# The last keys of two head groups as one pass of 64x32 tiles in an attention and feed-forward kernel

## The chip, the cores and the metric

The kernel runs on one core of a Trainium2 chip. The metric is the device time of one execution in microseconds, the median of several runs. The core has five engines that run their own queues in order and meet at semaphores: TensorE (PE) multiplies, VectorE (DVE) and ScalarE (ACT) work on tiles, GpSimd (POOL) issues most loads, SyncE (SP) issues most stores. TensorE writes its results to PSUM, which has eight banks here; the program calls them `banks`.

## The reference

```python
batch, n_heads, seq, head_dim = (8, 12, 448, 64)
scores = scale * np.matmul(q, k.transpose(0, 1, 3, 2))
scores = scores - np.max(scores, axis=-1, keepdims=True)
attn = np.exp(scores)
attn = attn / (np.sum(attn, axis=-1, keepdims=True) + 1e-09)
x = np.matmul(attn, v)          # then heads side by side: 3584 x 768
h = x @ w_in                    # 768 x 2048
g = h * (1.0 / (1.0 + np.exp(-h)))
return g @ w_out                # 2048 x 768
```

The sizes that matter below are the 448 keys of a head, which are three and a half chunks of 128, and the 448 queries, which are the columns that every attention matmul streams.

## The kernel before

**Units and pairs.** Four heads of one batch make a head group, `HG = 4`; each batch has three, so there are 24 units, numbered n. Units are taken in pairs (n, n+1), n even. For one unit the keys lie in chunks c = 0 to 3; the last chunk holds only 64 keys. The two units of a pair share it: unit n has its 64 keys on rows 0 to 63, unit n+1 on rows 64 to 127, and one exponentiated tile E holds both (`lead[n+1] = n` leads the second unit to the first one's tile).

**The attention work on TensorE.** A score pass (`scores`, recorded at L583) uses tiles of 32 rows and 128 columns of the array, one for each head, so four matmuls run side by side. The shared last chunk's scores (`scores_rest`) use 32x64 tiles, eight side by side. Sums and values (`attend`, L674 for the sums of a pair, L658 for values) use 128x32 tiles: four heads side by side, each on 32 columns of the array. I call a pass what runs side by side: four matmuls of 128x32 or 32x128, eight of 32x64, one of 128x128. A unit's value work is in two parts, one for the even and one for the odd elements of the head dimension; a part has four passes, one for each chunk, that add up in one bank. In the last of them the unit reads all 128 rows of the shared tile, and its V buffer holds zeros on the 64 rows that belong to the other unit. Those rows are cleared once per buffer by DVE (`clear_rows`, L468).

**The rest of TensorE's work.** The feed-forward products (`wide`, L573) use the full array, 128x128, or, while attention is still going on and the planner's clock is past `STRIPS`, four 128x32 strips for each product, so that they have the same tile size as the value passes. `FFN1_AT` is how many of the six passes of one first-layer product are put down at once before the planner looks for other work. From the middle of batch 4 on the first layer of two batches is done by a scheme with fewer products (L909); some weight combinations for it are made on DVE in good time (`TWB`, `SXB` are their priorities).

**Order.** The order of each engine's instructions is written out ahead of time by a planner, a small simulation (`Order`, and the loop at the end of `without_maximum`) with costs for each operation: a pass of n columns is n/2400 us plus 2.6 ns, a change of the array's tile size is `SWITCH = 0.104`. On TensorE it prefers a score pass if one is due and its spacing (`PACES`, one value for each unit) has elapsed; then any sum or value work that is ready; then feed-forward work. Right behind a score pass it puts all sum and value work that is ready:

```python
while n0 >= NG and (a := av_at()) is not None and a <= od.now:
    run_av()
```

Four of the eight banks are a ring `m_ring` that values, sums and feed-forward products share (the two scores in flight hold the other four). A value part takes one bank and gives it back when DVE has scaled it into xT (`norm`, L756). The E tiles are a ring of nine; a unit's are given back with its second value part. V buffers are a ring of four, given back at the same place, and POOL's next V load waits for that. The `B_...` values are priorities on ACT and DVE.

The sequence of sum and value operations of a pair is: the sums of both, then for unit n parts 1 and 2, then for unit n+1 parts 1 and 2:

```python
av_seq.append((ns, 0))
av_seq += [([n], part) for n in ns for part in (1, 2)]
```

Of the kernel before, what the change touches and what calls it, by code (L numbers as in the profile page):

```python
# [22 lines left out]
DMA_TAIL = 2.2  # L23
OPEN = 8
TS = (1, 3)
STRIPS = 50
W_LATE = 1.0
LAND = {1: -1.0, 2: -0.9, 3: -0.2, 4: 0.45, 5: 1.2, 6: 1.2, 7: 1.2, 8: 1.2, 9: 1.0, 10: 0.9, 11: 0.8, 12: 0.8}

# [1 line left out]
def mm(n):  # L31
    return n / 2400.0 + 0.0026
# [331 lines left out]
def without_maximum(  # L364
# [16 lines left out]
    HG = 4  # L381
# [11 lines left out]
    NT = 2 * S // 128  # L393
    OH = DM // 2
    NRK, NRQ, NKT, NV, NTH = 3, 4, 3, 4, 2
    PACES = (0.0, 0.0, 0.0, 1.6, 1.2, 2.0, 1.2, 1.2, 1.2, 1.2, 0.8, 1.8, 1.2, 1.2, 1.2, 1.2, 1.8, 1.8, 0, 0, 0.8, 0.8, 0.8, 2.5)
    B_TURN, B_ADD, B_GATE, B_TANH, B_WSUM, B_GSUM, B_FOURTH = 5, 5.5, -9, 11.2, 10, 2.5, 0
    B_NORM, B_INV, B_TAKE, B_READ = -10, -10, 1, -3.5
    LONES = ()
    NPL = 4  # L400
    HALVES = 4
# [2 lines left out]
    MORE0 = 4  # L404
    COLD, FIRST = 8.5, 39
    SHY = 0.3
    TWB, SXB, FAR = 12, 4, 20
    NE, NX3, NT_ = 9, 8, 2
    NXT = 3 * NX3
    NSG, NTMP, NOST = 3, 3, 4  # L410
# [18 lines left out]
    def bank_m(*key):  # L429
        return bank_of(4 + spot[key])  # L430
# [28 lines left out]
    VS = [const.tile([128, HG, NCH, D], FP16, name=f"V{i}") for i in range(NV)]  # L459

    def clear_v(i):
        f = form(i // NG, i % NG)
        before = form((i - NV) // NG, (i - NV) % NG) if i >= NV + NG else None
        return f != "lone" and f != before and i < B * NG
# [35 lines left out]
    def form(b, hg):  # L500
        n = NG * b + hg
        if n in LONES:
            return "lone"
        return ("low", "high")[(n - sum(x < n for x in LONES)) % 2]
# [87 lines left out]
    def per_burst(n):  # L592
        return 1
# [19 lines left out]
    def rows_of(n, c):  # L613
        return KROWS[c] if form(*units[n][:2]) == "lone" else 128
# [35 lines left out]
    def attend_mm(a, n, part, c, h, k0, k1, e, start, stop):  # L650
        b, hg, g0, g1 = units[n]
        nq = 32 * (g1 - g0)
        at = nq * (c % per_burst(n))
        if part == 0:
            w = side[:, n % 2] if n < 4 and c == NCH - 1 else ones[k0:k1, :]
        else:
            w = v_of(b, hg)[k0:k1, h + HG * hg * (b == 0), c, part - 1 :: 2]
        nc.tensor.matmul(  # L658
            out=a[32 * h : 32 * (h + 1), 0:nq],
            lhsT=w,  # L660
            rhs=e[k0:k1, h, at : at + nq],
            start=start,
            stop=stop,
        )
# [17 lines left out]
    def attend(ns, part):  # L682
        if part == 0 and len(ns) == 2:
            attend_sums(ns)
            return
        for n in ns:
            a = bank_m("a", n, part)
            acc[(n, part)] = a
            if part == 0 and n in TS:
                for i, (w, e) in enumerate(  # L690
                    ((ones, T[n]), (side[:, n % 2], E[(lead.get(n, n), NCH - 1)]))
                ):
                    for h in range(HG):
                        nc.tensor.matmul(  # L694
                            out=a[32 * h : 32 * (h + 1), 0:S],
                            lhsT=w,
                            rhs=e[:, h, 0:S],
                            start=(i == 0),
                            stop=(i == 1),
                        )  # L700
                continue
            if part == 0 and n < FOLD:
                nq = 32 * (units[n][3] - units[n][2])
                for w in range(2):
                    kr = rows_of(n, 2 * w)
                    for h in range(HG):
                        nc.tensor.matmul(
                            out=a[32 * h : 32 * (h + 1), 0:nq],
                            lhsT=ones[0:kr, :],
                            rhs=T[n][0:kr, h, nq * w : nq * (w + 1)],  # L710
                            start=(w == 0),
                            stop=(w == 1),
                        )
                continue
            for c in range(NCH):
                e = E[(lead.get(n, n) if c == NCH - 1 else n, c // per_burst(n))]
                for h in range(HG):
                    attend_mm(a, n, part, c, h, 0, rows_of(n, c), e, c == 0, c == NCH - 1)

    def inverse(ns, step, i=0):  # L720
        g0, g1 = units[ns[0]][2:]
# [476 lines left out]
    inv_op, norm_op = [], []  # L1198
    quads, fourth, begun = [], [], []

    PROD_AT, FFN1_AT = 1, 2

    def in_parts(n, size, columns, emit, done, at=0):
        to = min(at + size, n)
# [411 lines left out]
    for ns in jobs:  # L1616
        if len(ns) == 1:
            split = ((0,), (1,)) if ns[0] < HALVES else ((0, 1),)
            qk_seq += [(ns, c, ys) for c in range(NCH // per_burst(ns[0])) for ys in split]
        else:  # L1620
            split = ((0,), (1,)) if ns[0] < HALVES else ((0, 1),)
            each = [[([n], c, ys) for c in range(NCH - 1) for ys in split] for n in ns]
            if ns[0] == 0 and len(split) == 2:
                each[0].sort(key=lambda x: x[2])
            if ns[0] < 4:
                qk_seq += each[0] + [(ns, 3, (0, 1))] + each[1]
                av_seq += [([n], part) for n in ns for part in range(3)]
                lead[ns[-1]] = ns[0]
                continue
            qk_seq += each[0] + each[1] + [(ns, 3, (0, 1))]  # L1630
        av_seq.append((ns, 0))
        av_seq += [([n], part) for n in ns for part in (1, 2)]
        lead[ns[-1]] = ns[0]
    pace = {"next": 0.0}
    av_data = {"at": None}
# [97 lines left out]
    def av_at():  # L1733
        if not av_seq:
            return None
        ns, part = av_seq[0]
        if len(ns) == 2 and part == 0:
            if any(len(t_op.get(n, ())) < 2 or len(exp_op[n]) < 8 for n in ns):
                return None
            deps = [t_op[ns[0]][1], (t_op[ns[1]][1], mm(S))]  # L1740
            deps += [(x, 2 * mm(S)) for x in exp_op[ns[0]][6:8]]
            at, m = when(deps), m_ring.when(1)
            av_data["at"] = at
            return None if at is None or m is None else max(at, m)
        deps, b = [], units[ns[0]][0]
        for n in ns:
            if len(exp_op.get(n, ())) < 2 * NCH // per_burst(n):
                return None
            nq = 32 * (units[n][3] - units[n][2])
            if part == 0 and n in TS:  # L1750
                if len(t_op.get(n, ())) < 2:
                    return None
                deps += t_op[n] + [(x, mm(nq)) for x in exp_op[n] if x not in own_exp(n)]
                continue
            if part == 0 and n < FOLD:
                if len(t_op.get(n, ())) < 2:
                    return None
                deps += [t_op[n][0], (t_op[n][1], mm(nq))]
                continue
            made = exp_op[n][2:] + exp_op[n][:2] if n in (1, 3) else exp_op[n]  # L1760
            for i, x in enumerate(made):
                c = i // 2 * per_burst(n)
                deps.append((x, c * mm(nq)))
            if part:
                deps += [(x, LATE * (b == 0)) for x in ld_v[units[n][:2]]]
                if b > 0:
                    deps += [(x, 1.2) for x in rdn_op.get(n, [None])]
        at = when(deps)
        av_data["at"] = at
        m = m_ring.when(len(ns))  # L1770
        if at is None or m is None:
            return None
        return max(at, m)

    def run_av():
        ns, part = av_seq.pop(0)
        b, hg, g0, g1 = units[ns[-1]]
        nq = 32 * (g1 - g0)
        two = len(ns) == 2
        spot[("a", ns[0], part)] = m_ring.take()[0]  # L1780
        if part == 0:
            mms = 3 if two else 2 if ns[0] < FOLD or ns[0] in TS else 4
        else:
            mms = 4
        op = Op(
            "PE",
            mms * mm(nq) + 0.013,
            lambda: attend(ns, part),
            tail=PE_OUT,
        )  # L1790
        if part == 2:

            def then(at):
                n = ns[0]
                for _ in range(NCH // per_burst(n) - (lead.get(n + 1) == n)):
                    e_ring.give(at)
                b, hg = units[n][:2]
                if b:
                    v_ring.give(at)
                i = NG * b + hg + NV  # L1800
                if b and i < B * NG and clear_v(i):
                    od.add(Op("DVE", 0.2, lambda: clear_rows(i), [op], 5))

            op.then = then
        elif part == 0 and (two or ns[0] < FOLD or ns[0] in TS):
            op.then = lambda at: [t_ring.give(at) for _ in ns]
        od.on_pe(op, "cols")
        if part == 0:
            after_sums(ns, op, nq)
        else:  # L1810
            for n in ns:
                after_av(n, part, op, nq)
# [161 lines left out]
```

## Time and profile before

| | before |
|---|---|
| median of 3 runs | 383.17 us (383.01 to 383.21) |
| the profiled execution | 382.61 us |
| its span | 381.1 us |
| PE busy | 374.5 us, 98% |
| DVE busy | 280.7 us, 74% |
| ACT busy | 257.6 us, 68% |
| granted TensorE clock | 0.997 |
| score passes L583 | 768 matmuls |
| value matmuls L658 over E and V | 672 |

In the lists of the profile a row is one stretch of instructions of the same line and operands: when it starts, how long it lasts, engine, line, operation, what it writes and reads, the tile of the array (rows x columns, as in 128*32), the operand, and how many there are. The ends of matmuls are modelled, so durations overlap the next row; what a stretch costs is read from start to start.

### The profile page before, as it was taken

What the parts mean: (1) busy time and instruction counts of PE and PEld (TensorE: products, weight loads), DVE (VectorE), ACT (ScalarE), POOL (GpSimd) and SP (SyncE); (2) the same over time, 40 slices, a digit from 0 to 9 for tenths busy, and PEclk for the clock granted to TensorE, in tenths of its full rate; (3) what the DMA queues carried; (4) which work ended last, traced back from release to release, by engine and by line L of the source; (5) the groups of instructions that cost most, each with busy time, mean ns of one, the idle gap of its engine ahead of it and who ended that gap; (6) DMA issues with size and microseconds to landing.
All of it is one profiled execution on the core that took longest, in us unless ns stands there. A gap on an engine that the chain in (4) does not pass through costs nothing.

```text
span 381.1 us, 12970 instructions
## 1 busy us (share of the span) xinstructions
PE 374.5 (98%) x5516; PEld 192.7 (51%) x5516; DVE 280.7 (74%) x562; ACT 257.6 (68%) x425; POOL 91.0 (24%) x160
## 2 busy tenths in 40 slices
PE   8999999999999999999999999999999999999994
PEld 6433455444555444445544454555555555556553
DVE  5679799999996868996879978889876334656441
ACT  4998854787867797967788786738762259882221
POOL 7527515406042603324240500030001000000000
PEclk9999999999999999999999999999999999999998
DMA  7999999936558743739491702120002330001433
GB/s 109 202 206 196 185 210 183 154 74 94 74 98 134 137 71 46 103 76 170 81 143 26 98 23 67 34 54 0 1 7 70 83 93 2 0 1 45 107 80 109
DMA packets 35999, 34.73 MB, mean 91 GB/s; under 512 B 12000, under 2 KB 35168, under 8 KB 35936
## 3 DMA queue, kind: packets, MB, share of 16 engines
q0 software_dynamic: 25232, 22.82, 40.4%
q1 hardware_dynamic: 10176, 10.53, 10.4%
q8 instruction: 45, 0.74, 0.8%
q10 hardware_dynamic: 528, 0.49, 0.5%
q14 instruction: 18, 0.15, 0.1%
HBM read 45.61 MB, written 11.01 MB: 149 GB/s over the span
## 4 chain that ended last, share of the span: by engine, by line
PE 95%; ACT 3%; DVE 1%; DMA 1%; issue 0%
PE banks L573 54%; PE banks L909 15%; PE banks L583 11%; PE banks L658 10%; ACT E L621 2%; PE banks L1853 2%; PE banks L979 2%; PE banks L674 2%; DMA out_dram<-ost 1%; DVE T L632 0%; PE banks L694 0%; DVE ost L1061 0%; DVE ost L1052 0%; ACT ost L1050 0%; DVE zeros L436 0%
## 5 line engine op out<-in xcount | busy, mean ns | idle before, releaser
L621 ACT ACTIVATE E<-banks 128x896 f16<-128x896 f32 x168 | 144.0, 919 | 41.1 <-PE banks L583 40.8
L573 PE MATMUL banks<-xT,w_in_t 128*32 128x448 f16 (+1 forms) x1446 | 90.5, 353 | 0.0
L573 PE MATMUL banks<-w_out_t,G 128*32 128x384 f16 (+1 forms) x968 | 67.4, 327 | 0.0
L573 PEld LDWEIGHTS <-G 128*32 128x32 f16 (+1 forms) x1240 | 47.0, 97 | 34.0 <-issue 6.5
L573 PEld LDWEIGHTS <-w_in_t 128*32 128x32 f16 (+1 forms) x1446 | 42.2, 97 | 43.2 <-issue 12.7
L519 POOL DMA_DIRECT2D V<-in_v_dram x84 | 46.0, 559 | 56.6 <-PE banks L658 42.9
L583 PE MATMUL banks<-rq,KT 32*128 32x448 f16 (+1 forms) x768 | 52.4, 363 | 0.3 <-ACT E L621 0.2
L782 ACT ACTIVATE th<-banks 128x448 f16<-128x448 f32 x72 | 37.1, 552 | 15.1 <-PE banks L573 13.2
L820 DVE SCALAR_TENSOR_TENSOR G<-th,banks 128x448 f16<-128x448 f16 (+1 forms) x72 | 39.8, 572 | 4.8 <-ACT th L782 4.5
L1043 ACT COPY ost<-banks 128x384 f32<-128x384 f32 x41 | 19.8, 485 | 33.1 <-PE banks L573 17.9
L573 PE MATMUL banks<-D,S 128*32 128x384 f16 (+1 forms) x544 | 38.1, 327 | 0.0
L942 ACT ACTIVATE G<-banks 128x448 f16<-128x448 f32 (+3 forms) x72 | 33.8, 553 | 5.3 <-DVE banks L925 3.5
L658 PE MATMUL banks<-E,V 128*32 128x448 f16 x672 | 35.7, 353 | 0.0
L756 DVE SCALAR_TENSOR_TENSOR xT<-banks,rdn 128x448 f16<-128x448 f32 x48 | 29.2, 618 | 5.6 <-PE banks L658 3.0
L925 DVE TENSOR_TENSOR banks<-banks,q 128x448 f32<-128x448 f32 x28 | 17.6, 633 | 15.7 <-PE banks L909 14.5
L573 PEld LDWEIGHTS <-S 128*32 128x32 f16 (+1 forms) x544 | 20.6, 97 | 14.7 <-issue 3.1
L496 POOL DMA_DIRECT2D rq<-in_q_dram x25 | 13.9, 557 | 58.9 <-PE banks L583 46.9
L632 DVE TENSOR_TENSOR T<-E,E 128x1792 f16<-128x1792 f16 x22 | 23.8, 1080 | 5.6 <-ACT E L621 5.5
L632 DVE TENSOR_TENSOR T<-T,E 128x1792 f16<-128x1792 f16 x22 | 23.9, 1085 | 5.2 <-ACT E L621 5.1
L583 PEld LDWEIGHTS <-KT 32*128 32x128 f16 (+1 forms) x768 | 12.4, 96 | 29.9 <-issue 27.2
L658 PEld LDWEIGHTS <-V 128*32 128x32 f16 x672 | 17.0, 97 | 16.0 <-issue 3.9
L909 PEld LDWEIGHTS <-w_in_t 128*128 128x128 f16 x168 | 16.4, 98 | 15.2
(163 smaller groups left out, 409.3 us busy)
## 6 DMA issues: line engine op xcount, KB each, us to landing
out_dram<-ost SPq DMA_DIRECT2D x200, 48.0 KB, 1.6
rk<-in_k_dram POOLq DMA_DIRECT2D x23, 224.0 KB, 5.8
rq<-in_q_dram POOLq DMA_DIRECT2D x23, 224.0 KB, 5.2
w_out_t<-in_moe_w_out_dram POOLq DMA_DIRECT2D x4, 768.0 KB, 13.1
V<-in_v_dram POOLq DMA_DIRECT2D x42, 64.0 KB, 4.4
V<-in_v_dram POOLq DMA_DIRECT2D x42, 48.0 KB, 4.6
w_in_t<-in_moe_w_in_dram POOLq DMA_DIRECT2D x3, 512.0 KB, 10.8
w_in_t<-in_moe_w_in_dram POOLq DMA_DIRECT2D x6, 256.0 KB, 6.3
```

The source lines that it names most:

```text
L519: nc.gpsimd.dma_start(out=v_of(b, hg0)[32 * x : 32 * (x + 1), at, 0:count, :], in_=v[b, hs].rearrange("h (i g) d -> i h g d", g=TPP)[:, :, ...
L573: nc.tensor.matmul(out=out[at], lhsT=lhsT[:, at], rhs=rhs, **flags)
L583: nc.tensor.matmul(out=pS[p0 : p0 + 32 * (x1 - x0), h % 2, at : at + nq], lhsT=KT[(b, hg)][32 * h : 32 * (h + 1), c, x0:x1, :, e], rhs=QT[ ...
L621: nc.scalar.activation(out=E[(n, w)][0:kr, 2 * y : 2 * y + 2, 0:nk], in_=pS_t[(n, w, y)][0:kr, :, 0:nk], func=AF.Exp, scale=attn_scale,)
L632: nc.vector.tensor_tensor(out=T[n], in0=T[n] if step else E[(n, 0)], in1=E[(n, step + 1)], op=ALU.add,)
L658: nc.tensor.matmul(out=a[32 * h : 32 * (h + 1), 0:nq], lhsT=w, rhs=e[k0:k1, h, at : at + nq], start=start, stop=stop,)
L756: nc.vector.scalar_tensor_tensor(out=x3(b, cc)[:, cc % 3, 32 * g0 : 32 * g1], in0=acc[(n, part)][:, 0:nq], scalar=0.5, in1=rdn_t[n].rearra ...
L782: nc.scalar.activation(out=th, in_=h_t[(b, f, t0)][:, 0 : t1 - t0], func=AF.Tanh)
L820: nc.vector.scalar_tensor_tensor(out=dst[:, f, at + lo : at + hi], in0=th_t[(b, f, t0)][:, lo - t0 : hi - t0], scalar=1.0, in1=h_t[(b, f, ...
L909: nc.tensor.matmul(out=pp_t[(f, PBANK[m])], lhsT=w[:, c, :], rhs=a[:, c, :], start=(c == 0 and m in (1, 6, 5)), stop=(c == 2), skip_group_ ...
L942: nc.scalar.activation(out=o, in_=a, func=AF.Silu, scale=2.0)
L1043: nc.scalar.copy(out=ost(qd, i, j), in_=bank(qd, m))
```

## The change

For the pairs from unit 4 on, the shared last chunk is done once for both units. In each part the first operation, that of unit n, takes two banks, one for each unit, and begins with one pass of eight 64x32 tiles: rows 0 to 63 of the shared tile with V of unit n into unit n's bank, rows 64 to 127 with V of unit n+1 into unit n+1's bank, four heads each. Then come the three full chunks of unit n. The operation of unit n+1 has its three full chunks alone, and adds to the bank that is already begun. The order of a pair becomes part 1 of n and n+1, then part 2 of n and n+1; the E tiles that each gives back are four for unit n and three for n+1, where they were three and four. The V buffers of these units need no zeros, so `clear_v` leaves them out. The planner's op for the first unit costs one `SWITCH` more. Besides, `STRIPS` goes from 50 to 58, `FFN1_AT` from 2 to 1, and the spacings and priorities are other numbers, so the order as a whole is drawn anew.

```diff
-STRIPS = 50
+STRIPS = 58
...
-    PACES = (0.0, 0.0, 0.0, 1.6, 1.2, 2.0, 1.2, 1.2, 1.2, 1.2, 0.8, 1.8, 1.2, 1.2, 1.2, 1.2, 1.8, 1.8, 0, 0, 0.8, 0.8, 0.8, 2.5)
-    B_TURN, B_ADD, B_GATE, B_TANH, B_WSUM, B_GSUM, B_FOURTH = 5, 5.5, -9, 11.2, 10, 2.5, 0
-    B_NORM, B_INV, B_TAKE, B_READ = -10, -10, 1, -3.5
+    PACES = (0.0, 0.0, 0.0, 1.2, 2.0, 2.8, 2.8, 1.4, 1.4, 1.4, 1.4, 1.4, 1.4, 1.6, 0, 0, 1.8, 1.8, 1.8, 0.4, 0.4, 0.4, 0.4, 0)
+    B_TURN, B_ADD, B_GATE, B_TANH, B_WSUM, B_GSUM, B_FOURTH = 5, -0.5, -9, 15.2, 10, 2, 0.5
+    B_NORM, B_INV, B_TAKE, B_READ = -10, -10, 13.5, -7.5
...
-    TWB, SXB, FAR = 12, 4, 20
+    TWB, SXB, FAR = 0, 0, 20
...
     def clear_v(i):
+        if i >= 4:
+            return False
...
-            for c in range(NCH):
-                e = E[(lead.get(n, n) if c == NCH - 1 else n, c // per_burst(n))]
+            if n < 4:
+                for c in range(NCH):
+                    e = E[(lead.get(n, n) if c == NCH - 1 else n, c // per_burst(n))]
+                    for h in range(HG):
+                        attend_mm(a, n, part, c, h, 0, rows_of(n, c), e, c == 0, c == NCH - 1)
+                continue
+            if n not in lead:
+                acc[(n + 1, part)] = bank_m("a", n + 1, part)
                 for h in range(HG):
-                    attend_mm(a, n, part, c, h, 0, rows_of(n, c), e, c == 0, c == NCH - 1)
+                    for i in range(2):
+                        attend_mm(
+                            acc[(n + i, part)], n + i, part, NCH - 1, h,
+                            64 * i, 64 * (i + 1), E[(n, NCH - 1)], True, False,
+                        )
+            for c in range(NCH - 1):
+                for h in range(HG):
+                    attend_mm(a, n, part, c, h, 0, 128, E[(n, c)], False, c == NCH - 2)
...
-    PROD_AT, FFN1_AT = 1, 2
+    PROD_AT, FFN1_AT = 1, 1
...
-        av_seq += [([n], part) for n in ns for part in (1, 2)]
+        av_seq += [([n], part) for part in (1, 2) for n in ns]
...
-        m = m_ring.when(len(ns))
+        first = part and ns[0] >= 4 and ns[0] not in lead
+        second = part and ns[0] >= 4 and ns[0] in lead
+        m = 0.0 if second else m_ring.when(2 if first else len(ns))
...
-        spot[("a", ns[0], part)] = m_ring.take()[0]
+        first = part and ns[0] >= 4 and ns[0] not in lead
+        second = part and ns[0] >= 4 and ns[0] in lead
+        if not second:
+            spot[("a", ns[0], part)] = m_ring.take()[0]
+        if first:
+            spot[("a", ns[0] + 1, part)] = m_ring.take()[0]
...
-            mms = 4
+            mms = 3 if second else 4
...
-            mms * mm(nq) + 0.013,
+            mms * mm(nq) + 0.013 + SWITCH * bool(first),
...
-                for _ in range(NCH // per_burst(n) - (lead.get(n + 1) == n)):
+                count = NCH // per_burst(n) - (lead.get(n + 1) == n)
+                for _ in range(count if n < 4 else 4 - (n in lead)):
```

More of the change, by code (lines that the diff above doesn't have):

```diff
@@ L1760, in av_at @@
             made = exp_op[n][2:] + exp_op[n][:2] if n in (1, 3) else exp_op[n]
+            if part and n >= 4 and n not in lead:
+                made = exp_op[n][6:8] + exp_op[n][:6]
+                deps += ld_v[units[n + 1][:2]]
+            elif part and n >= 4:
+                made = [x for x in made if x in own_exp(n)]
             for i, x in enumerate(made):
```

## The prediction

> **What bounds the kernel now.** I read the page's busy times and chain first, then TensorE's waits, then two stretches of TensorE's list in order of time. Busy shares and chain:
>
> ```profile
> PE 374.5 (98%) x5516; PEld 192.7 (51%) x5516; DVE 280.7 (74%) x562; ACT 257.6 (68%) x425; POOL 91.0 (24%) x160
> PE 95%; ACT 3%; DVE 1%; DMA 1%; issue 0%
> L658 PE MATMUL banks<-E,V 128*32 128x448 f16 x672 | 35.7, 353 | 0.0
> ```
>
> TensorE is the chain. Who it waited for:
>
> ```profile
> PE banks L1853 <- DVE zeros L436: 1.2, 1, 1.2
> PE banks L694 <- DVE T L632: 0.3, 1, 0.3
> PE banks L583 <- ACT E L621: 0.2, 1, 0.2
> ```
>
> It waits 1.7 us in all, every one of them before 33 us. So the time after that is TensorE's passes plus what lies between them, and only a change of these two sums moves the end, unless the new order brings waits. The stretch around 104 us is a typical pair:
>
> ```profile
> 100.98 0.61 PE L583 MATMUL banks<-rq,KT 32*64 32x448 f16 x16
> 101.53 2.30 PE L573 MATMUL banks<-w_out_t,G 128*32 128x384 f16 x52
> 103.75 0.58 PE L583 MATMUL banks<-rq,KT 32*128 32x448 f16 x8
> 104.26 0.56 PE L674 MATMUL banks<-T,half 128*32 128x448 f16 x8
> ...
> 104.84 1.47 PE L573 MATMUL banks<-w_out_t,G 128*32 128x384 f16 x32
> 106.14 0.93 PE L658 MATMUL banks<-E,V 128*32 128x448 f16 x16
> 107.00 0.57 PE L583 MATMUL banks<-rq,KT 32*128 32x448 f16 x8
> 107.50 0.67 PE L573 MATMUL banks<-w_out_t,G 128*32 128x384 f16 x12
> 108.00 0.93 PE L658 MATMUL banks<-E,V 128*32 128x448 f16 x16
> 108.76 0.98 PE L573 MATMUL banks<-w_out_t,G 128*32 128x384 f16 x20
> 109.68 0.57 PE L583 MATMUL banks<-rq,KT 32*128 32x448 f16 x8
> 110.18 1.70 PE L658 MATMUL banks<-E,V 128*32 128x448 f16 x32
> ```
>
> And the stretch that the move of `STRIPS` touches:
>
> ```profile
> 49.77 2.08 PE L573 MATMUL banks<-xT,w_in_t 128*32 128x448 f16 x40
> 51.67 0.55 PE L674 MATMUL banks<-T,half 128*32 128x448 f16 x8
> ...
> 52.24 2.44 PE L573 MATMUL banks<-xT,w_in_t 128*32 128x448 f16 x48
> 54.51 3.20 PE L658 MATMUL banks<-E,V 128*32 128x448 f16 x64
> 57.54 1.47 PE L573 MATMUL banks<-w_out_t,G 128*32 128x384 f16 x32
> ```
>
> Three prices come out of the starts. A pass of 448 columns: 64 value matmuls are 16 passes and last from 54.51 to 57.54, 3.03 us, so 0.189 us each. No change of tile: the strips at 104.84 are 8 passes of 384 columns, 8 x 0.1626 = 1.30 us, and the values start at 106.14, just 1.30 us later; strips and values follow each other free. A change of tile: from 106.14 to 107.00 are four passes, 0.757 us, and 0.10 more; from 107.00 to 107.50 are two passes, 0.379, and 0.12 more; from 100.98 to 101.53 two passes of eight 32x64 tiles, 0.379, and 0.17 more. Doing the same for every change in the trace, without those where TensorE waited, I get as medians 0.115 us from 128x32 to 32x128 (59 cases) and 0.112 to 32x64 (10), 0.126 from 32x128 to 128x32 (60), 0.153 from 32x64 to 128x32 (11), and 0.116 from 128x32 to 128x128 (3).
>
> **The change part by part.** *Passes taken away.* A pair now needs 1 + 3 + 3 passes in each part where it needed 4 + 4. That the eight tiles run side by side in one pass is shown for 32x64 tiles by the 100.98 row (16 matmuls in two passes' time). Ten pairs (units 4 to 23) times two parts is 20 passes, 20 x 0.1893 = 3.79 us less, all on TensorE's path. The number of value matmuls stays 672.
>
> *Changes of tile added.* Each of the 20 passes of 64x32 stands between others: it is entered by a change and left by a change to 128x32. No such change is in the trace. Below, the price of one can't be under zero, which would need the two row heights to mix freely; above, the largest clean ones are 0.153 to enter and 0.181 to leave. Every change that the trace has, also the one that alters only the column width (128x32 to 128x128, 0.116), costs over 0.10, so I take the nearest rows: to enter from 128x32, 0.112 (to eight tiles); to leave, 0.153 (from eight tiles). One pass so costs 0.265 when it stands behind strips, sums or values, more than the 0.189 it saves. Behind a score pass it costs less: the change from 32x128 was to be paid anyhow (0.126, and I take the same into 64x32), so only the 0.153 is new, and 0.036 is won.
>
> How many stand behind scores? In the trace the ten pairs' value work lies in 21 stretches. The first stretch of a pair starts behind a score pass in 2 of 10 (209.27 and 229.58 us); the rows at 106.14 and 108.00 start behind strips, that at 110.18 behind scores. Of the 11 further stretches 8 start behind scores. The new part 2 of unit n needs two free banks of four while part 1 still holds two and the feed-forward at least one, so it will start a stretch of its own, once DVE has scaled part 1's banks (L756, 618 ns each). I give it 7 of 10. So 9 of 20 stand behind scores and 11 don't: 11 x 0.265 + 9 x 0.153 = 2.92 + 1.38 = 4.29 us more.
>
> The Trainium skill, "TensorE: Matmul & The Clock Gate", section "Part 3: Packing small matmuls", gives about 4 ns more for each further tile that runs side by side. By it, as an estimate, leaving eight tiles costs 0.126 + 4 x 0.004 = 0.142 where this trace's row has 0.153, and the 20 exits would be 0.2 us cheaper, a sum of 383.8; the row decides.
>
> *STRIPS from 50 to 58.* In the stretch shown, sums and values of the first pair lie among strips without a change. With full-array products there are changes: into the sums (no clean row for 128x128 to 128x32; I take 0.11, between 0.105 from 128x128 to 32x128 and 0.116 the other way), out of them 0.116, and out of the values 0.116; the entry into the values is the 64x32 entry counted above. Leaving the 32x64 scores for 128x128 instead of strips would save about 0.02. Sum 0.32 us more, or nothing if the new order does these after 58 us.
>
> *Banks, E tiles, V buffers.* The first E tiles come back with part 2 of unit n, which is now the third operation. At 106.14 the two first operations would last 4 x 0.189 + 0.265 = 1.02 and 0.57 us, then about 0.9 for two banks, then 1.02: ready at 109.65 instead of 108.76. The score pass behind it in the trace is at 109.68, so nothing is late; if it were, ACT's exponentials (L621, two of 919 ns for a score pass) would start up to 0.9 us later, and ACT is busy 38.9 of the 50 us from 100 to 150, so it has some 4 us to spare in a pair's 20. TensorE has feed-forward passes to put in the gap. V loads on POOL wait for the same operation (L519, 42.9 us idle for L658), and the K and Q loads behind them in POOL's queue wait too; they land 4.4 to 5.8 us after issue for units two pairs later, some 40 us, so a delay of 0.9 us is covered. SP's stores move with their products alone.
>
> *Zeros.* Three of the four memsets of V go (165 ns each, 0.5 us). DVE makes them at 2.28 us and then idles 1.06 us for the first keys at 4.48: nothing. If the keys came earlier, 0.5 us of the start would be won.
>
> *FFN1_AT, spacings, priorities.* `FFN1_AT` splits no pass, and TensorE is full either way: nothing. The number of score passes, 70 from unit 4 on, is fixed, and both pairs of score banks are used by each, so two can't lie side by side: their changes stay. The first three spacings are zero in both, so the start to 28 us, where TensorE fills with zeros, stays. From there to 33 us are some 0.5 us of waits that another order could win. I take zero for the redraw, with +2.5 us (a late release of 0.25 us in each of the ten pairs) and -0.5 us as ends.
>
> **Sum:** -3.79 + 4.29 + 0.32 = +0.82 us. The profiled execution took 382.61, 1.5 around its span of 381.1; it would take 383.4. The median of the runs shown is 0.56 above that execution, so for the median 383.17 + 0.82 = 384.0.
>
> **The rivals.** *A change of row height alone is cheap.* 64x32 and 128x32 tiles use the same column groups; if the array need not come to rest between them, the price s of one change falls. The cost is 11 x 2s + 9s = 31s, and with 0.32 the change breaks even at s = 0.112; under 0.087 it is faster by over 0.2% (0.77 us, which is about what a measurement of this kernel can tell from no change). At s = 0.05 the time is 383.17 - 3.79 + 1.55 + 0.32 = 381.3, at zero 379.7. For it: the planner counts one change where two are needed behind strips. Against: every change of size in the trace costs 0.10 or more, whichever dimension it is. The Trainium skill, "TensorEngine Tiling (Array Packing)", section "Tiling Modes", says that every change of tiling mode drains the array. By that rule both changes count, as in the sum; no run here shows it yet for 64x32.
>
> *The redraw lays the passes well.* If all 20 stand behind scores and the first pair comes after 58 us: 20 x 0.153 - 3.79 = -0.73, so 382.4. Against: 2 of 10 first parts do so now, since the first part is released by DVE's reciprocals.
>
> *The redraw brings waits.* The order is fixed, so a score pass put before its banks are free stops TensorE. At 0.25 us in each of ten pairs beside the sum: 386.5. For it: DVE is busy 47.7 of the 50 us from 50 to 100, and two banks at once are harder to get than one. Against: TensorE now waits nowhere after 33 us.
>
> **How the numbers follow.** The forecast (prices as in the rows, no new waits) has 0.52; its own range runs from 383.3 (prices 0.02 lower, no cost of `STRIPS`) to 385.0 (all 20 behind strips: 20 x 0.265 - 3.79 + 0.32 = +1.83), and it straddles the 0.2% bound at 383.94: 0.28 slower, 0.24 within. Cheap changes 0.25, all faster. Well laid 0.10: 0.07 faster, 0.03 within. Waits 0.13, slower. Together: faster 0.32, same 0.27, slower 0.41. The range goes from 380.8 (s = 0.035) to 385.9 (the forecast with most of the waits), leaving out a tenth at each end.
>
> **What would show it.** In the profile after: value matmuls as 160 of 64*32 and 512 of 128*32; from the start of a 64x32 stretch to the next start 0.34 us if leaving costs 0.153, 0.19 if it is free; the strips or values before them 0.11 over their passes; some 60 fewer matmuls in all from `STRIPS`; TensorE's waits still 1.7 us. I am wrong if the start-to-start of a 64x32 pass is under 0.25 us, if most of these passes stand behind scores, or if TensorE shows waits on L621, L756 or L820 after 33 us.

## The result and the profile after

The changed kernel took 384.0 us (median of 10 runs, 383.46 to 385.79), the kernel before 382.98 (10 runs, 382.48 to 383.43). The ratio is 1.0035, with an interval of 1.002 to 1.005: slower by 0.35%, 0.8 to 1.9 us. The profiled execution took 383.69 us around a span of 382.1, 1.08 more than the one before.

The page's busy times and the group of value matmuls, after:

```profile
PE 375.5 (98%) x5510; PEld 188.9 (49%) x5510; DVE 280.6 (73%) x559; ACT 258.0 (68%) x425; POOL 90.2 (24%) x160
L660 PE MATMUL banks<-E,V 128*32 128x448 f16 (+1 forms) x672 | 34.9, 356 | 0.0
```

TensorE is still busy 98% of the span, and the value matmuls are still 672. Its waits:

```profile
PE banks L1881 <- DVE zeros L436: 1.2, 1, 1.2
PE banks L585 <- ACT E L623: 0.2, 1, 0.2
PE banks L575 <- DVE X L835: 0.2, 1, 0.2
```

The last one is new: at 70 us a feed-forward pass waits for a gate that VectorE makes late. The one on T at 33 us is gone. TensorE's list around the same pair as before:

```profile
107.18 1.64 PE L575 MATMUL banks<-w_out_t,G 128*32 128x384 f16 x36
108.75 1.64 PE L660 MATMUL banks<-E,V 64*32 64x448 f16 x32
110.21 1.15 PE L575 MATMUL banks<-w_out_t,G 128*32 128x384 f16 x24
111.29 1.64 PE L660 MATMUL banks<-E,V 64*32 64x448 f16 x32
```

A row of 32 value matmuls begins with the eight 64x32 ones; the rest are 24 of 128x32. Nine strips passes from 107.18 are 1.46 us and end at 108.64, so the change into 64x32 costs 0.11. From 108.75 to 110.21 are 1.46 us, of which seven passes are 1.325; the change out of 64x32 so costs 0.13, and from the start of a 64x32 pass to the next start it is 0.314 us. Over all twenty such passes the medians are 0.113 to enter from 128x32 (14 of them), 0.103 from 128x128 (2), 0.126 from the 32x128 scores (4), and 0.125 to leave. And the stretch that STRIPS touches:

```profile
49.21 2.25 PE L575 MATMUL banks<-xT,w_in_t 128*128 128x448 f16 x11
51.39 0.56 PE L676 MATMUL banks<-T,half 128*32 128x448 f16 x8
...
52.08 2.06 PE L575 MATMUL banks<-xT,w_in_t 128*128 128x448 f16 x10
54.07 1.63 PE L660 MATMUL banks<-E,V 64*32 64x448 f16 x32
55.64 0.55 PE L575 MATMUL banks<-xT,w_in_t 128*128 128x448 f16 x2
```

Eleven passes from 49.21 end at 51.29, so 0.10 into the sums; 0.12 out of them and 0.12 out of part 1 of the values: in all 0.33 us (0.34 by these rounded figures).

The sum of the whole trace, start to start, against the one before: passes -3.79; entries 14 x 0.113 + 2 x 0.103 = +1.79, the four behind scores 0.50 instead of 0.50; exits +2.72, of which 0.23 is a longer one at 256 us, where the two parts of the last pair follow each other; STRIPS +0.33; the stretch at 70 us +0.41; the lost wait at 31.7 us -0.36; the start, with its fill of zeros, -0.14. That is +0.96 of the 1.00 us by which the last matmul ends later; the work after it adds 0.08.

### The profile page after: what moved, and what is told of

Same layout as the page of the kernel before. It is cut to its first block, busy times and chain, and to the rows that moved or that the text cites. A ratio compares the mean times of both kernels' runs of the same rounds, so it can differ in the third digit from the quotient of the medians.

```text
span 382.1 us, 12947 instructions
## 1 busy us (share of the span) xinstructions
PE 375.5 (98%) x5510; PEld 188.9 (49%) x5510; DVE 280.6 (73%) x559; ACT 258.0 (68%) x425; POOL 90.2 (24%) x160
## 4 chain that ended last, share of the span: by engine, by line
PE 91%; DMA 3%; ACT 2%; DVE 2%; POOL 0%; issue 0%; POOLq 0%
PE banks L575 52%; PE banks L924 15%; PE banks L585 11%; PE banks L660 10%; DMA rq<-in_q_dram 2%; ACT E L623 2%; PE banks L994 2%; PE banks L676 2%; DMA out_dram<-ost 1%; DVE D L822 0%; DVE w_out_t L822 0%; PE banks L1881 0%; DVE rq L568 0%; POOL rk L490 0%; DVE G L835 0%
## 5 line engine op out<-in xcount | busy, mean ns | idle before, releaser
L575 PE MATMUL banks<-xT,w_in_t 128*32 128x448 f16 (+1 forms) x1440 | 91.5, 353 | 0.0
L797 ACT ACTIVATE th<-banks 128x448 f16<-128x448 f32 x72 | 38.1, 552 | 10.1 <-PE banks L575 9.5
L835 DVE SCALAR_TENSOR_TENSOR G<-th,banks 128x448 f16<-128x448 f16 (+1 forms) x72 | 40.0, 569 | 5.7 <-ACT th L797 5.5
L957 ACT ACTIVATE G<-banks 128x192 f16<-128x192 f32 (+3 forms) x72 | 33.7, 552 | 5.7 <-DVE banks L940 2.8
L660 PE MATMUL banks<-E,V 128*32 128x448 f16 (+1 forms) x672 | 34.9, 356 | 0.0
L771 DVE SCALAR_TENSOR_TENSOR xT<-banks,rdn 128x448 f16<-128x448 f32 x48 | 28.2, 617 | 3.7 <-PE banks L660 3.0
L660 PEld LDWEIGHTS <-V 128*32 128x32 f16 (+1 forms) x672 | 13.9, 95 | 19.3 <-issue 12.4
```

Source lines behind the costliest of these rows:

```text
L575: nc.tensor.matmul(out=out[at], lhsT=lhsT[:, at], rhs=rhs, **flags)
L660: nc.tensor.matmul(out=a[32 * h : 32 * (h + 1), 0:nq], lhsT=w, rhs=e[k0:k1, h, at : at + nq], start=start, stop=stop,)
L771: nc.vector.scalar_tensor_tensor(out=x3(b, cc)[:, cc % 3, 32 * g0 : 32 * g1], in0=acc[(n, part)][:, 0:nq], scalar=0.5, in1=rdn_t[n].rearra ...
L797: nc.scalar.activation(out=th, in_=h_t[(b, f, t0)][:, 0 : t1 - t0], func=AF.Tanh)
L835: nc.vector.scalar_tensor_tensor(out=dst[:, f, at + lo : at + hi], in0=th_t[(b, f, t0)][:, lo - t0 : hi - t0], scalar=1.0, in1=h_t[(b, f, ...
L957: nc.scalar.activation(out=o, in_=a, func=AF.Silu, scale=2.0)
```

## The experiments

The times of all kernels here, the one before too, vary by 1 to 3 us from run to run, the kernel before once by 5. Part of it is the start: the first pair's sums begin at 51.39 us in one profile and at 52.05 or 54.07 in others of the same first instructions, when the q loads land later. So below, where less than 1 us matters, I also read a stretch that lies behind the start: from the first sum matmul of pair (6, 7) to the end of the last matmul. Two profiles of the changed kernel give 294.47 us for it both times.

### The changed kernel again, with full rows, and with nothing

The first is the changed kernel itself. The second keeps its order of instructions and replaces the eight 64x32 tiles by two 128x32 passes:

```diff
-                for h in range(HG):
-                    for i in range(2):
+                for i in range(2):
+                    for h in range(HG):
                         attend_mm(
                             acc[(n + i, part)], n + i, part, NCH - 1, h,
-                            64 * i, 64 * (i + 1), E[(n, NCH - 1)], True, False,
+                            0, 128, E[(n, NCH - 1)], True, False,
                         )
```

(with the zero rows of V made again). The third leaves the loop out, and the first full chunk starts the sum in the bank.

> The changed kernel itself, on one chip with the next three, as their yardstick. Theory (the 20 passes of 64x32 tiles cost what their changes of tile cost, 0.113 to enter from 128x32, 0.125 to leave): 1.0 us over the kernel before, as recorded. Its ten runs spread from 383.46 to 385.79 where the kernel before spreads from 382.48 to 383.43; rival for that spread, and for part of the loss: the wait at 70 us, where TensorE stands 0.23 us for a gate that VectorE makes late after a q load, is longer in some runs. Then the runs that are over 384.5 would show TensorE waiting 1 us or more between 60 and 75 us.

> The changed kernel with its order untouched, but each pass of eight 64x32 tiles replaced by two passes of 128x32 tiles over all 128 rows, with the other unit's rows of V zero, as before the change. Theory (changes of tile): 20 more passes at 0.189 are 3.79 us more, 16 entries at 0.113 and 20 exits at 0.125 fall away, 4.3 us less: 0.5 us faster than the changed kernel, TensorE's list free of gaps at these places. Rival (the passes of 64x32 are a gain and the redrawn order is what costs): slower than the changed kernel by 1.5 to 3.8 us.

> The changed kernel in its own order with the 20 passes of 64x32 tiles left out: the values of the shared last keys are missing from the output. Theory: 20 x 0.189 of passes and 4.3 us of changes of tile go, 8.1 us less than the changed kernel, 0.40 us for each pass. Rival (the array needs no rest between the two row heights): 3.8 us less, 0.19 for each.

Measured on one chip beside 383.24 for the kernel before (23 runs): again 384.12 (12 runs, ratio 1.0025, 1.0011 to 1.004), full rows 384.12 (12 runs, ratio 1.0028, 1.0014 to 1.0041), none 378.81 (4 runs, ratio 0.987, 0.985 to 0.989). The changed kernel is again 0.9 us slower, with 1.0 expected. The list with full rows, at the same place:

```profile
108.31 1.31 PE L573 MATMUL banks<-w_out_t,G 128*32 128x384 f16 x28
109.44 1.69 PE L658 MATMUL banks<-E,V 128*32 128x448 f16 x32
110.96 1.15 PE L573 MATMUL banks<-w_out_t,G 128*32 128x384 f16 x24
```

and with none:

```profile
109.54 1.31 PE L660 MATMUL banks<-E,V 128*32 128x448 f16 x24
110.67 1.15 PE L575 MATMUL banks<-w_out_t,G 128*32 128x384 f16 x24
```

Full rows follow the strips without a gap, 1.52 us for eight passes. With the 64x32 pass it was 0.11 + 1.46 = 1.57, with none it is 1.13. So the pass with its two changes is worth 0.44 here, and the two passes that it replaces 0.39. Over the stretch from pair (6, 7) on, with 18 such passes, full rows take 294.15 us, 0.32 less than the changed kernel; none takes 288.22, 6.25 less, and it has a wait of its own of 1.1 us on xT in it, so 7.35 / 18 = 0.41 for each. My expectation was 0.40, and 0.19 if the array needed no rest. The time of the whole kernel fell by 5.3 us and not by the 8.1 that I had expected: in the profile of that run TensorE also waits 1.9 us for q, and the changed kernel's first profile has neither wait. So the price rests on the lists, not on this time. For the whole kernel I had expected 0.5 less with full rows; the times of these two don't differ, the trace says 0.3. Place by place the two lists of this stretch agree with the prices: full rows gain 0.05 us at each of the 14 passes behind strips, sums or values and lose 0.065 at each of the four behind scores, some 0.4 in all. They give back 0.17 at 233 us, where their values take that much longer with no wait on record, and gain 0.08 more at the last pair. The rival by which the tiles gain and the order loses (1.5 to 3.8 slower with full rows) is out.

On the spread: in the second profile of the changed kernel, of a run of 384.24 us, TensorE waits 0.8 us for q and 0.4 for the gate at 70 us, so these two waits vary from run to run. But the kernel before spreads on this chip from 382.16 to 384.8, no less than the changed one, so the spread is not the change's. No run over 384.5 of the changed kernel has a profile, so what makes those stays open.

### The new numbers without the tiles, the tiles without the new numbers

One kernel is the one before with only STRIPS, FFN1_AT, PACES, the `B_` values and TWB, SXB of the change; the other is the change with all of these as before.

> The kernel before with the changed kernel's numbers alone (STRIPS 58, FFN1_AT 1, spacings and priorities), no 64x32 tiles, the old sequence of parts. Theory: only STRIPS costs, 0.3 us by three changes of tile, so 383.0 to 383.6. Rival (the redraw brings waits): 384 or more with TensorE waiting on VectorE or ScalarE after 33 us.

> The changed kernel's 64x32 passes and sequence of parts with the numbers of before (STRIPS 50, FFN1_AT 2, the old spacings and priorities). Here 18 of the 20 passes stand behind strips, sums or values and 2 behind scores. Theory (0.113 to enter, 0.125 to leave, 0.189 saved): 18 x 0.113 + 20 x 0.125 - 3.79 = 0.75 us over the kernel before if the order brings no waits. Rival (the tiles gain and the redraw loses): at least 1.5 us under the kernel before.

The new numbers alone: 385.74 us against 383.24 (6 runs, ratio 1.0076, 1.0059 to 1.0094). The tiles alone: 392.21 against 382.97 (5 runs, ratio 1.0243, 1.0218 to 1.0268). Both theories of mine fell here, and so did the rival of the second, by which the tiles gain. The new numbers around the old passes bring this wait, at 278 us:

```profile
PE banks L909 <- DVE banks L925: 1.4, 1, 1.4
```

That is the rival in that expectation, and 1.4 + 0.33 are most of the 2.5. The tiles with the old numbers show two things. At the pair (8, 9), in TensorE's list:

```profile
107.78 0.58 PE L585 MATMUL banks<-rq,KT 32*128 32x448 f16 x8
...
111.49 1.63 PE L660 MATMUL banks<-E,V 64*32 64x448 f16 x32
...
117.02 1.63 PE L660 MATMUL banks<-E,V 64*32 64x448 f16 x32
118.58 0.57 PE L585 MATMUL banks<-rq,KT 32*128 32x448 f16 x8
```

and before the last pair:

```profile
255.74 0.57 PE L585 MATMUL banks<-rq,KT 32*128 32x448 f16 x6 [0.44 <-ACT E L623]
257.14 0.39 PE L585 MATMUL banks<-rq,KT 32*64 32x448 f16 x4 [0.82 <-ACT E L623]
```

Part 2 of unit 8 comes 5.5 us after part 1, and between two score passes, 107.78 and 118.58, lie 10.8 us without one. Most of the delay arises at this one pair: the sums of the next one, (10, 11), start at 132.4 us, where they start at 123.0 in the kernel before, and those of the last pair at 258.5 instead of 245.6. Feed-forward work is used up early, and at the end scores and values stand alone and wait for ScalarE's exponentials one after another. In the stretch from 240 to 265 us and in its last five (busy time of PE, PEld, DVE, ACT, POOL, then the granted clock, the DMA share and GB/s) it shows as idle time and as a lower clock, which was 1.00 from 240 to 265 us before:

```profile
240.00:265.00 25.00, 22.32 (x386) 8.88 (x379) 20.43 (x37) 17.90 (x26) 0.16 (x1) 0.93 0.08 19
260.00:265.00 5.00, 4.81 (x68) 1.82 (x68) 4.93 (x9) 1.63 (x3) 0.16 (x1) 0.72 0.02 3
```

The lower clock fits a loss that the recorded waits don't hold: the values that start at 260.68 us are 14 passes and four changes of tile, 3.1 us by the prices above, and take 4.1.

### One bank or two

What holds part 2 back? Either the two banks that its first operation must get at once, or the new sequence of parts, or the tiles. Two kernels with the old numbers and no 64x32 tile tell them apart: one has the sequence with a bank for each operation, as before; the other has the order of the tiles alone, two banks at once, with two full-row passes for each 64x32 pass (the loop of the full rows above). The core of the first, against the changed kernel:

```diff
-        m = 0.0 if second else m_ring.when(2 if first else len(ns))
+        m = m_ring.when(len(ns))
...
-                count = NCH // per_burst(n) - (lead.get(n + 1) == n)
-                for _ in range(count if n < 4 else 4 - (n in lead)):
+                for _ in range(NCH // per_burst(n) - (lead.get(n + 1) == n)):
```

> The kernel before with the changed sequence of parts alone (part 1 of both units, then part 2 of both), 128x32 passes over zero rows, the old numbers, each value part taking one bank for itself. Theory (what made the tiles with the old numbers 9 us slower is that their first operation must get two banks at once, which holds back the pair, its E tiles and so the next score passes, until the feed-forward work runs out before the last pair): here no two banks are asked for, so 383 to 385, and no waits of over 1 us between 250 and 265 us. Rival (the sequence of parts, which gives E tiles back later): about 392, with these waits.

> The order that the changed tiles get with the old numbers, with the first operation taking two banks, but each 64x32 pass replaced by two passes of 128x32 over zero rows; no 64x32 tile in it. Theory (two banks): within 1 us of the 392.2 that the tiles took with the old numbers, with TensorE idle around 250 to 265 us. Rival (the 64x32 passes themselves): under 386.

One bank: 383.69 us against 382.99 (10 runs, ratio 1.001, 0.998 to 1.004). Two banks: 391.82 (4 runs, ratio 1.020, 1.013 to 1.027). Both came as the theory had it. TensorE's score passes with one bank, at the same pair:

```profile
107.99 0.57 PE L583 MATMUL banks<-rq,KT 32*128 32x448 f16 x8
...
112.34 0.57 PE L583 MATMUL banks<-rq,KT 32*128 32x448 f16 x8
```

No gap of 10 us, and after 34 us a single wait, of 0.5. With two banks, at this pair:

```profile
108.30 0.57 PE L583 MATMUL banks<-rq,KT 32*128 32x448 f16 x8
...
111.90 1.69 PE L658 MATMUL banks<-E,V 128*32 128x448 f16 x32
...
117.36 1.70 PE L658 MATMUL banks<-E,V 128*32 128x448 f16 x32
118.99 0.57 PE L583 MATMUL banks<-rq,KT 32*128 32x448 f16 x8
```

The two parts again lie 5.5 us apart, and the score passes 10.7. TensorE waits 2.4 us for exponentials, as with the tiles themselves. So it is not the tiles and not the sequence; it is the demand for two banks or what goes with it in the planner (four and three E tiles given back instead of three and four, and other costs of the two operations), which was not tried by itself. The count of E tiles is the less likely of these, since with two banks the earlier operation gives back four and not three. How the demand holds part 2 back is inferred: with the tiles, DVE had scaled both banks of part 1 by 113.9 us, and until 117.02 TensorE ran feed-forward products, which take the ring's banks one at a time. No view shows who holds a bank.

### STRIPS back at 50

```diff
-STRIPS = 58
+STRIPS = 50
```

> The changed kernel with STRIPS back at 50, the rest as changed. Theory: three changes of tile between 50 and 58 us go, 0.33 us less than the changed kernel; the wait near 70 us on VectorE stays. Rival (STRIPS is what costs the redraw its 0.7 us over the tiles): as fast as the kernel before.

383.98 us against 382.97 (10 runs, ratio 1.0032, 1.0015 to 1.0048). By the times it can't be told from the changed kernel. In the profile the last matmul ends at 376.77 us instead of 377.28, 0.51 earlier, and TensorE has no wait on X at 70 us. That fits the 0.33 and the missing wait, which I had expected to stay, but a single profile of another order is weak support. The rival, as fast as before, is out by the interval.

### The passes laid behind score passes

The planner holds a ready 64x32 pass back while a score pass can start soon, and keeps the last free E tiles for such score passes:

```diff
-            if qk is not None and qk <= od.now and (od.now >= pace["next"] or moe_i is None):
+            held = av is not None and av <= od.now and qk_seq and shared_next()
+            if qk is not None and qk <= od.now and (
+                held or moe_i is None or (od.now >= pace["next"] and not kept())
+            ):
...
-                if av is not None and av <= od.now - 0:
+                if av is not None and av <= od.now and not (qk_seq and shared_next() and soon_qk(qk)):
```

> The changed kernel with STRIPS 50 and a planner that puts 64x32 passes right behind score passes: it holds a ready one back while a score pass can start within 1 us, and it saves the last free E tiles for score passes that go ahead of them. 15 of 20 then stand behind scores, where 4 did. Theory: 11 x 0.113 = 1.24 less for the entries and 0.33 for STRIPS: 1.5 us under the changed kernel, some 0.5 us under the kernel before. Rival (a change into or out of 64x32 costs the same behind scores): not more than 0.4 under the changed kernel.

> The same planner rule with the numbers of before instead of the changed ones (STRIPS 50, FFN1_AT 2, old spacings and priorities); 15 of 20 passes behind scores. Theory: 5 x 0.113 + 20 x 0.125 - 3.79 = 0.72 us under the kernel before if the order brings no waits. Rival: the score passes that are held back leave ScalarE idle, the last pair ends 13 us later, and TensorE waits at the change to the next stage: slower than the kernel before.

395.09 us and 394.95 against 382.97 (5 runs each, ratio 1.031 for both): 11 us over the changed kernel where I had expected 1.5 under it, and the rival of the second expectation came true. The price came out as expected: 15 of 20 passes stand behind scores, and there the change from 32x128 into 64x32 is 0.125 where the change into 128x32 is 0.126, so the entry costs nothing more. In the list of one of them:

```profile
110.29 0.57 PE L585 MATMUL banks<-rq,KT 32*128 32x448 f16 x8
110.80 1.63 PE L660 MATMUL banks<-E,V 64*32 64x448 f16 x32
```

From 110.29 to 110.80 are two passes and 0.13. But the rule costs some ten times what it was to gain. Score passes that wait for value passes come late, the last pair's sums begin at 262.94 us instead of 247.46, and before that TensorE stands for ScalarE:

```profile
PE banks L585 <- ACT E L623: 4.8, 9, 0.9
```

Of these kernels none that computes the whole output is faster than the kernel before. Not tried was to put the 64x32 pass at the end of a stretch that a score pass follows: then unit n's scaling would have to wait for the second unit's passes too. Nor were the 64x32 passes of both parts laid back to back, so that one entry and one exit serve two of them; they would take all four banks of the ring.

## Why the prediction was right or wrong

**The bound.** Right: TensorE is busy 98% in both, and nearly all of the difference is passes and changes of tile on it.

**Passes taken away.** Right: 20 passes, 3.79 us; the eight tiles run side by side.

**Price of a change.** Right that both the entry and the exit cost over 0.10, so that the cheap-change rival is out (0.41 for each pass with its changes where that rival gives 0.19). The Trainium skill, "TensorEngine Tiling (Array Packing)", section "Tiling Modes", has every change of mode drain the array. This trace agrees in that a change of row height alone has a price, 0.113 and 0.125; the draining itself is not seen in it. The entry was right, 0.112 against 0.113. The exit was mis-sized: I took 0.153 from the 32x64 row, and it measured 0.125. That row holds two passes, and the price of leaving it was counted from its first. By the starts of the single matmuls in the trace of the kernel before, the second pass of such a row starts 0.226 us after the first, 0.037 more than a pass of 448 columns takes (11 rows); from the second to the next tile's start it is one pass and 0.117. The row of 32x128 tiles divides in the same way: of its 0.126, 0.022 lie between its two passes (56 rows) and 0.105 behind the second. What lies between the passes is no change of tile, and why it is there stays open. A 64x32 pass stands alone, so the part to compare with is 0.117, against 0.125. The Trainium skill, "TensorE: Matmul & The Clock Gate", section "Part 3: Packing small matmuls", gives about 4 ns for each further tile side by side. Put on 0.126 that gave 0.142, too much; put on 0.105 it gives 0.121, as an estimate, and this trace agrees, with 0.117 and 0.125 for eight tiles.

**How many stand behind scores.** Wrong: I gave 9 of 20, there are 4. Part 1 of unit n came behind scores in 1 of 10 where I had 2, part 2 in 3 of 10 where I had 7. I took part 2's share from the later stretches of the kernel before. Part 2 does start a stretch of its own in nine of the ten pairs, as I said, but six of these begin behind feed-forward work.

These two errors cancel. My term for the changes was 4.29 us; with the measured prices and counts it is 1.79 + 2.49 = 4.28. The total is as good as it is by that chance. The rest nearly cancels too: 0.23 for the longer exit at 256 us, 0.41 at 70 us, -0.36 at 31.7 us and -0.14 at the start.

**STRIPS.** Right: 0.32 forecast, 0.33 in the trace: into the sums, out of them, and out of part 1 of the values. The 0.02 that I took off for leaving the 32x64 scores did not come (0.156 there, 0.161 in the kernel before). By the times alone it could not be confirmed.

**Banks, E tiles, V buffers.** In the changed kernel the step held at the pair I had worked it out for: part 2 starts 2.54 us behind part 1 (108.75 and 111.29), where 1.02 + 0.57 + 0.9 = 2.49 were expected. As a statement about the change it failed: it looked at one pair, and took the two banks to be got within about 0.9 us. With the old numbers and nothing else different, part 2 of the same pair came 5.5 us after part 1, the next score pass came only behind that, and the kernel lost 9 us. That the score pass waited for E tiles is inferred from the planner's rules. The changed kernel is spared this by its numbers.

**FFN1_AT, spacings, priorities.** "Nothing" was right only for the pair that was put together: 0.41 us lost at 70 us, 0.23 of it a recorded wait, and 0.36 won at 31.7. Each by itself is no neutral: with the old passes the new numbers cost 2.5 us, the old numbers with the new passes 9. My ends of +2.5 and -0.5 held for the first and not for the second. Which of the numbers does it was not tried.

**Zeros.** Right: three of the memsets are gone, and the first score pass starts at 5.78 where it was at 5.82.

**The signs.** The value matmuls are 160 and 512 as I had said, and 0.314 us from a 64x32 start to the next lies nearer the 0.34 of a full price than the 0.19 of a free one. One of the signs that I had named for being wrong did come: a wait on L820 (L835 in the changed kernel) after 33 us, of 0.23 us. The matmuls are 6 fewer and not 60: 20 products that ran on the full array at 252.87 us, behind the last pair's values, now run as strips ahead of them. And the lower end of the forecast's own range, 383.3, takes 0.02 off each pass; off each change of tile it is 383.05.

## What to carry to other kernels

A tile shape that halves a pass has to pay for two changes of tile: 0.113 + 0.125 us here against a pass of 0.189, so a pass that stands alone pays only where one of the changes is due anyway. A price for a change that is read from a row of several passes should be counted from the row's last pass. Where an order is drawn by a planner, a change of what an operation holds (here two banks at once instead of one) can cost far more than what the operation itself saves; test the order with the old arithmetic and the old order with the new, since each of them alone may lose where both together look neutral. And before a sum that came out right is believed, its terms should be read off one by one.

## What the runs showed that I had not expected

The second of two passes of score tiles starts late without any change of tile: by 0.037 us for 32x64 tiles and 0.022 for 32x128, while value passes of 128x32 follow each other at 0.189 us. And when TensorE stood for exponentials between 250 and 263 us, the granted clock fell to 0.93 over the stretch from 240 to 265 us with the tiles alone, and to 0.72 over its last five, where it is 1.00 over the stretch in the kernel before.
